# Value products of heads 25 to 27 in one stretch, in the load with the last K but one

## The chip, the core and the metric

The kernel runs on one NeuronCore of one Trainium2 chip. The metric is device time in microseconds (us) of one execution; lower is better. Five engines work side by side, each through its own list of instructions in program order: PE (TensorE, matrix products into PSUM; "PEld" is its weight load), DVE (VectorE, element-wise work and reductions), ACT (ScalarE, copies and activations), POOL (GpSimd, reductions over partitions) and SP (SyncE, which here only issues the DMA transfers). Semaphores make an instruction wait for another engine or for a transfer.

## The reference

One decode step for two batch rows: attention over the last 2048 positions of a KV cache with 32 heads of 128, plus a gated feed-forward block, both on the same normalised input. Cut to what matters:

```python
# B=2, Sq=1, D=512, 32 heads, Dh=128, W=2048 cached positions used, F=1376
xn = layernorm(x)
q  = (xn @ wq)                                  # per head 128 numbers
scores = einsum("bhqd,bhkd->bhqk", q, k) * Dh**-0.5
p  = softmax(scores)
o  = einsum("bhqk,bhkd->bhqd", p, v)            # "PV"
A  = o.reshape(B, 1, 32*128) @ wo
Bf = ((xn @ w_gate) * (xn @ w_up)) @ w_down
out = x + A + Bf
```

All data are float32. Nearly all bytes are K and V: 2 MB for each of K and V of one head, 159.5 MB in all. Each byte is used once.

## The kernel before

**The stream.** The host lays everything out as one stream, in the order in which the kernel reads it. `blocks()` cuts the stream into loads. A large load fills one of three SBUF buffers of 128 x 15872 words (`step0`, `step1`, `step2`; in the rows also `step_49`, `step_50`, `step_51`), and the loads take the buffers in turn. SP issues the transfers into a buffer when everything that lay there has been used (`done` counts the fields of a load, `pump` issues the next). Each transfer waits only for the instructions that touched the columns that it writes. All transfers are in SP's one list, in order.

**The loads that matter here.** They are the last ones of the stream:

- the load in `step1` with K of heads 28 and 29, and among others the first five eighths of V of head 25;
- the load in `step2` with K of head 30 ("the load with the last but one K"): the last three eighths of V of head 25, `wo` of head 25, V and `wo` of heads 26 and 27;
- the load in `step0` with K of head 31, V and `wo` of head 28, and two pieces of `w_down`;
- into `step1`, two transfers of 2304 KB: V and `wo` of head 29, then V and `wo` of head 30;
- into `step2`, four transfers: V of head 31 (2048 KB, over the columns of K of head 30), `wo` of head 31 with three pieces of `w_down` (1024 KB, over the last V of head 25 and `wo` of head 25), and two more with the rest of `w_down` (512 and 256 KB, over V of head 26).

**One head.** DVE multiplies K by the broadcast query (`products`) and reduces (`sums`, `maxima`); POOL takes the maximum over partitions; ACT makes the exponentials (`weights`, tile `p`, six buffers); POOL sums them; DVE takes the reciprocal. On PE then come three steps, which the text calls PV, pick and wo:

- **PV** (`weigh`): eight matmuls per head, 16 columns of weights, 512 columns of V each. Four of them write four different 32-row groups of one PSUM bank, so four can run at once. There are two banks, `o_ps0` and `o_ps1`, used in turn. Two heads can share a bank (heads 23 and 24 before, 26 and 27 here); head 25 is by itself. `copy_out` lets ACT copy the bank to SBUF (`o_sb`, two buffers).
- **pick** (`transpose`): four matmuls that turn `o_sb` and pick each head's rows, with only 2 or 4 moving columns against 128 x 128 weights, into PSUM tile `tr`; ACT then scales the result by the reciprocal into `oT` (four buffers). All picks share one PSUM bank, so a pick waits until ACT has read the one before.
- **wo** (`project_o`): one matmul of 512 columns into the sum `acc`.

A matmul in float32 is two instructions in the trace, so eight matmuls of PV are "x16" there.

**Filler.** `keep_busy(n)` is a matmul of n columns on fixed data into a PSUM bank that nobody reads (`spare`, which is the bank `q0`). It computes nothing. It stands where PE would otherwise wait for ACT.

**What sets the order.** Each engine runs its instructions in the order in which the code writes them. For the load with the last but one K, `values()` is called twice: on head 25's fields, then on those of heads 26 and 27. It runs PV as V's fields come, and at the end of a bank's last head copies out, picks and, when `wo` is there, projects. Behind it come, in program order: the maximum of head 30 (DVE), the product of head 31's K (DVE), PV of head 28, two matmuls of `w_down` (`down(1)`), a copy of the sum `acc` to SBUF (`acc_sb`, DVE), the sums of head 31 (DVE), pick of head 28, a filler, the copied sum put back into four row groups (`accumulate(carry, acc_sb)`), wo of head 28 in four matmuls of 128 columns, then heads 29, 30 and 31 one after the other, and the rest of `w_down`. The lines of `before.py` that call these, with H = 32 and GC = 512:

```python
last_two = [f for f in fields if f[1] in (H - 6, H - 5) or f[0] == "vp" and f[1][0] >= H - 6]
values([f for f in fields if f not in last_two])      # head 25
values(last_two, ((GC, 256), (GC,)))                  # heads 26, 27, with filler
keep_busy(GC)
...
transpose([HF], o_sb)                                 # head 28
keep_busy(256)
accumulate(carry, acc_sb)
project_o(HF)
```

All engine calls go through one helper, so every instruction of the profile has the line L243; they are told apart by tile names.

Of the kernel before, what the change touches and what calls it, by code (L numbers as in the profile page):

```python
# [15 lines left out]
B, D, H, DH, SK, F = 2, 512, 32, 128, 8192, 1376  # L16
# [15 lines left out]
GC = HG * DH  # L32
# [6 lines left out]
NV = CK // FB  # L39
# [232 lines left out]
def sliding_attention_plus_glu_kernel(  # L272
# [20 lines left out]
    tiles, used, left, got = {}, {}, {}, {}  # L293
# [3 lines left out]
    def pump():  # L297
        while todo:
            key, fields, at = todo[0]
            if key not in tiles:  # L300
                if key[0] == "f":
                    n = sum(w for _, _, w in fields)
                    tiles[key] = flow.tile([P, n], "first")
                elif not slots:
                    return
                else:
                    tiles[key] = slots.pop(0)
                used[key] = 0
            todo.pop(0)
            c0 = used[key]  # L310
            for kind, i, w in fields:
                got[kind, i] = (tiles[key][:, used[key] : used[key] + w], key)
                used[key] += w
            c1 = used[key]
            src = stream[at : at + P * pitch(fields)].rearrange("(p i) -> p i", p=P)
            sp.dma_start(tiles[key][:, c0:c1], src[:, : c1 - c0])

    def done(kind, i):
        _, key = got.pop((kind, i))
        left[key] -= 1  # L320
        if left[key] == 0 and key[0] != "f":
            slots.append(tiles.pop(key))
            pump()
# [61 lines left out]
    q_ps, s_t, mm_t, p_t, sum_t, rec_t, o_sbs, oT = {}, {}, {}, {}, {}, {}, {}, {}  # L385
# [8 lines left out]
    def side(h):  # L394

        return int(h % 3 == 0)
# [43 lines left out]
    def sums(h):  # L440
        s_t[h] = flow.ring([P, B, J], "s", 6)
        dve.tensor_reduce(s_t[h], k_of(h), axis=AX.X, op=ALU.add)
        done("k", h)

    def maxima(h):
        s = s_t[h]
        m = flow.ring([P, B], "m", 6)
        dve.tensor_reduce(m, s, axis=AX.X, op=ALU.max)
        mm = flow.ring([P, B], "mm", 6)
        pl.partition_all_reduce(mm, m, P, bass_isa.ReduceOp.max)  # L450
        mm_t[h] = mm
# [20 lines left out]
    def accumulate(lhsT, rhs, last=False):  # L472
        nonlocal n_acc
        for g in range(4):
            pe.matmul(
                acc_g[32 * g : 32 * g + M, :], lhsT, rhs[:, g * P : (g + 1) * P],
                start=(n_acc == 0), stop=last,
            )
        n_acc += 1

    def keep_busy(n):
        pe.matmul(spare[:, 0:n], mean_w, spare_in[:, 0:n], start=True, stop=True)

    def weigh(h, v, parts, first, last):


        for n, part in enumerate(parts):
            b, i = divmod(part, JG)
            pe.matmul(
                o_ps[bank][32 * i : 32 * i + 8 * B, :], p_t[h][:, b, i, :],  # L490
                v[:, FB * n : FB * (n + 1)], start=first and b == 0, stop=last and b == B - 1,
            )

    def copy_out():
        nonlocal bank
        o_sb = flow.ring([P, 4 * DH], "o_sb", 2)
        act.copy(o_sb, o_ps[bank])
        bank = 1 - bank
        return o_sb

    def transpose(heads, o_sb):
        d = tr[:, 8 + 4 * bank : 12 + 4 * bank]
        s0, s1 = side(heads[0]), side(heads[-1]) + 1
        dst = d.rearrange("p (s b) -> p s b", b=B)[:, s0:s1, :]
        for r in range(4):
            pe.matmul(
                dst, o_sb[:, r * DH : (r + 1) * DH], pick[:, r, s0:s1, :],
                start=(r == 0), stop=(r == 3),
            )
        for h in heads:  # L510
            rec = rec_t.pop(h)
            oT[h] = oT_ring[h % 4]
            for b in range(B):
                c = B * side(h) + b
                act.activation(
                    oT[h][:, RB * b : RB * b + 1], d[:, c : c + 1], AF.Copy,
                    scale=rec[:, b : b + 1],
                )

    def project_o(h):  # L520
        wo = got["wo", h][0]
        if h < HF:
            pe.matmul(acc, oT.pop(h), wo, start=(h == 0), stop=False)
        else:
            accumulate(oT.pop(h), wo)
        done("wo", h)
# [12 lines left out]
    def values(fields, busy=((), ())):  # L539
        for kind, i, _ in fields:  # L540
            if kind == "vp":
                h, p0, p1 = i
                heads = next(g for g in groups if h in g)
                weigh(h, got[kind, i][0], range(p0, p1), h == heads[0], h == heads[-1])
                done(kind, i)
                if (h, p1) == (heads[-1], NV):
                    o_sb = copy_out()
                    for n in busy[0]:
                        keep_busy(n)
                    transpose(heads, o_sb)  # L550
                    for n in busy[1]:
                        keep_busy(n)
                    ready.extend(heads)
            elif kind == "wo":
                arrived.append(i)
            while ready and ready[0] in arrived:
                project_o(ready.pop(0))
# [103 lines left out]
    spare, o_ps2 = spare_t[:, 0, :], spare_t[:, 1, :]  # L661
    products(h)
    sums(h)
    last_two = [f for f in fields if f[1] in (H - 6, H - 5) or f[0] == "vp" and f[1][0] >= H - 6]
    values([f for f in fields if f not in last_two])
    values(last_two, ((GC, 256), (GC,)))
    keep_busy(GC)
    maxima(h)
    reciprocals(h - 1)
    products(h + 1)  # L670
# [4 lines left out]
    dve.tensor_copy(acc_sb, acc)  # L675
    sums(h + 1)
    transpose([HF], o_sb)
    keep_busy(256)
    accumulate(carry, acc_sb)
    project_o(HF)  # L680
    weights(h)
# [14 lines left out]
    for k, t in enumerate((o_ps[bank], o_ps2)):  # L696
        for n in range(CK // FB):
            b, i = divmod(n, JG)
# [113 lines left out]
```

## Time and profile before

| | us |
|---|---|
| median of three runs | 381.35 |
| lowest and highest run | 380.67, 382.10 |
| the profiled execution's own time | 381.04 |
| its span, first to last instruction | 379.7 |
| PE busy | 261.7 (69%) |
| DVE busy | 295.2 (78%) |
| ACT busy | 58.2 (15%) |
| DMA engines, mean busy share of the queue that carries the stream | 97.4% |

The span is what the trace covers; the rows' times count from its start. The execution's own time is 1.34 us longer than its span (381.04 - 379.7). A row of a timeline or of the chain reads: start, duration, engine, tile that is written, and how many instructions were merged; in brackets the idle time just before and what ended it. In a table of stretches "PEclk" is the share of full speed that the TensorE clock was granted.

### The profile page before, as it was taken

What the parts mean: (1) busy time and instruction counts of PE and PEld (TensorE: products, weight loads), DVE (VectorE), ACT (ScalarE), POOL (GpSimd) and SP (SyncE); (2) the same over time, 40 slices, a digit from 0 to 9 for tenths busy, and PEclk for the clock granted to TensorE, in tenths of its full rate; (3) what the DMA queues carried; (4) which work ended last, traced back from release to release, by engine and by line L of the source; (5) the groups of instructions that cost most, each with busy time, mean ns of one, the idle gap of its engine ahead of it and who ended that gap; (6) DMA issues with size and microseconds to landing.
All of it is one profiled execution on the core that took longest, in us unless ns stands there. A gap on an engine that the chain in (4) does not pass through costs nothing.

```text
span 379.7 us, 2753 instructions
## 1 busy us (share of the span) xinstructions
PE 261.7 (69%) x1100; PEld 90.7 (24%) x1100; DVE 295.2 (78%) x147; ACT 58.2 (15%) x259; POOL 25.3 (7%) x78
## 2 busy tenths in 40 slices
PE   3167776895589168867775767880888184848997
PEld 3133124222133012211221212220222021203345
DVE  3069998992699992799999918999999099999460
ACT  1002012111021012111111111100212010201132
POOL 1000000000001000000000000000000000010010
PEclk9759696699688757886889687697689668566999
DMA  8999999999999999999999999999999999999991
GB/s 340 453 473 428 431 420 429 428 428 432 428 428 435 428 428 428 443 448 448 435 424 428 448 428 435 428 423 448 435 429 435 423 435 438 440 415 410 431 414 48
DMA packets 3950, 159.70 MB, mean 421 GB/s; under 512 B 466, under 2 KB 610, under 8 KB 994
## 3 DMA queue, kind: packets, MB, share of 16 engines
q1 hardware_dynamic: 3938, 159.54, 97.4%
q8 instruction: 8, 0.13, 0.1%
q14 instruction: 4, 0.03, 0.0%
HBM read 159.47 MB, written 0.07 MB: 420 GB/s over the span
## 4 chain that ended last, share of the span: by engine, by line
DMA 63%; PE 21%; DVE 14%; ACT 2%; issue 0%; SPq 0%
DMA step<-in_stream_dram 63%; PE o_ps L243 7%; DVE s L243 7%; DVE step L243 7%; PE q L243 6%; PE acc L243 4%; PE tr L243 3%; ACT o_sb L243 1%; ACT oT L243 1%; DVE m L243 0%; SPq L243 0%; DVE o_out L243 0%; DVE rec L243 0%; SPq L242 0%
## 5 line engine op out<-in xcount | busy, mean ns | idle before, releaser
L243 DVE TENSOR_TENSOR step<-step,q 128x4096 f32<-128x4096 f32 x31 | 136.7, 4411 | 47.3 <-DMA step<-in_stream_dram 47.3
L243 DVE TENSOR_REDUCE s<-step 128x32 f32<-128x4096 f32 x32 | 141.4, 4419 | 1.1
L243 PE MATMUL q<-step,xnb 128*128 128x512 f32 (+1 forms) x128 | 80.1, 773 | 72.6 <-DMA step<-in_stream_dram 72.6
L243 PE MATMUL o_ps<-step,p 128*16 128x512 f32 (+1 forms) x512 | 106.1, 764 | 10.2 <-DMA step<-in_stream_dram 10.2
L243 PEld LDWEIGHTS q<-step,xnb 128*128 128x128 f32 x128 | 28.7, 242 | 117.2 <-DMA step<-in_stream_dram 81.4
L243 PE MATMUL acc<-step,oT 128*9 128x512 f32 (+1 forms) x88 | 42.0, 638 | 9.1 <-ACT oT L243 9.1
L243 PE MATMUL tr<-first,o_sb 128*128 128x2 f32 (+2 forms) x198 | 29.8, 269 | 18.2 <-ACT o_sb L243 12.7
L243 PEld LDWEIGHTS o_ps<-step,p 128*16 128x16 f32 x512 | 18.8, 108 | 81.7 <-issue 69.2
L243 PEld LDWEIGHTS tr<-first,o_sb 128*128 128x128 f32 x198 | 27.6, 210 | 42.6 <-ACT o_sb L243 34.9
L243 ACT COPY o_sb<-o_ps 128x512 f32<-128x512 f32 (+1 forms) x24 | 13.8, 576 | 130.8 <-PE o_ps L243 130.8
L243 POOL PARTITION_ALL_REDUCE mm<-m x32 | 11.3, 354 | 266.5 <-DVE m L243 256.6
L243 ACT ACTIVATE nm<-mm 128x2 f32<-128x2 f32 x32 | 6.5, 203 | 142.1 <-POOL mm L243 142.1
L243 ACT ACTIVATE p<-s,nm 128x16 f32<-128x16 f32 x64 | 19.2, 300 | 1.0
L243 POOL PARTITION_ALL_REDUCE sum<-rs x32 | 12.7, 398 | 76.8 <-ACT p L243 76.8
L243 ACT ACTIVATE oT<-tr,rec 128x1 f32<-128x1 f32 x64 | 12.2, 260 | 29.1 <-PE tr L243 29.1
L243 DVE TENSOR_TENSOR step<-step,tr 128x4096 f32<-128x4096 f32 x1 | 4.4, 4422 | 15.1 <-DMA step<-in_stream_dram 15.1
L243 ACT ACTIVATION_READ_ACCUMULATOR p<-s,nm 128x1 f32 x64 | 12.0, 187 | 0.0
L243 PE MATMUL o_ps<-step,xn 128*2 128x512 f32 (+1 forms) x48 | 10.5, 569 | 0.0
L243 PEld LDWEIGHTS acc<-step,oT 128*9 128x9 f32 x88 | 4.5, 94 | 20.9 <-ACT oT L243 15.2
L243 PE MATMUL q<-xnb,mean_w 128*128 128x512 f32 (+1 forms) x18 | 8.5, 563 | 0.0
L243 DVE TENSOR_REDUCE m<-s 128x2 f32<-128x32 f32 x32 | 5.9, 186 | 1.1
L243 DVE RECIPROCAL rec<-sum 128x2 f32<-128x2 f32 x32 | 5.0, 155 | 2.2 <-POOL sum L243 2.2
(43 smaller groups left out, 38.1 us busy)
## 6 DMA issues: line engine op xcount, KB each, us to landing
step<-in_stream_dram SPq DMA_DIRECT2D x14, 7936.0 KB, 36.0
step<-in_stream_dram SPq DMA_DIRECT2D x2, 7680.0 KB, 33.2
step<-in_stream_dram SPq DMA_DIRECT2D x1, 7872.0 KB, 58.2
step<-in_stream_dram SPq DMA_DIRECT2D x1, 7808.0 KB, 39.0
step<-in_stream_dram SPq DMA_DIRECT2D x1, 4864.0 KB, 30.3
step<-in_stream_dram SPq DMA_DIRECT2D x2, 2304.0 KB, 19.5
step<-in_stream_dram SPq DMA_DIRECT2D x1, 2048.0 KB, 18.2
step<-in_stream_dram SPq DMA_DIRECT2D x1, 1024.0 KB, 20.3
```

Source lines behind the costliest of these rows:

```text
L243: made = getattr(eng, method)(*args, **kwargs)
```

## The change

In the load with the last but one K, the two calls of `values` and the filler behind them are replaced by a loop written out:

- PV of head 25 (its last three eighths), of head 26 and of head 27 come one after the other. ACT still copies a bank out when its last head is through, now both copies before any pick of these heads.
- Pick of head 25 stands behind PV of head 27, then a filler of 256 columns, then pick of heads 26 and 27. Before, fillers of 512 and 256 columns stood ahead of the pick of heads 26 and 27, and one of 512 behind it.
- wo of heads 25, 26 and 27 come together, and a filler of 256 columns behind them where one of 512 stood.
- Behind pick of head 28 the filler of 256 columns goes.

```diff
     sums(h)
-    last_two = [f for f in fields if f[1] in (H - 6, H - 5) or f[0] == "vp" and f[1][0] >= H - 6]
-    values([f for f in fields if f not in last_two])
-    values(last_two, ((GC, 256), (GC,)))
-    keep_busy(GC)
+    o_sbs = []
+    for kind, i, _ in fields:
+        if kind == "vp":
+            g, p0, p1 = i
+            single = g == H - 7
+            weigh(g, got[kind, i][0], range(p0, p1), single or g == H - 6, single or g == H - 5)
+            done(kind, i)
+            if p1 == NV and g != H - 6:
+                o_sbs.append(copy_out())
+    transpose([H - 7], o_sbs[0])
+    keep_busy(256)
+    transpose([H - 6, H - 5], o_sbs[1])
+    for g in (H - 7, H - 6, H - 5):
+        project_o(g)
+    keep_busy(256)
     maxima(h)
...
     sums(h + 1)
     transpose([HF], o_sb)
-    keep_busy(256)
     accumulate(carry, acc_sb)
```

DVE's and SP's lists are the same before and after; POOL's too. Three places of the lists of PE and ACT show what moves.

PE, from the arrival of the load with the last but one K to PV of head 28, before (`p1`, `p2`, `p3` are the weights of heads 25, 26, 27; `oT1`, `oT2`, `oT3` their picked values; `q0<-xnb` is filler):

```order
L243 MATMUL o_ps1<-step2_51,p1_58 16x512 x3
L243 MATMUL tr<-first_52,o_sb1_117 128x2 x4
L243 MATMUL acc<-step2_51,oT1_64 9x512
L243 MATMUL o_ps0<-step2_51,p2_59 16x512 x8
L243 MATMUL o_ps0<-step2_51,p3_60 16x512 x8
L243 MATMUL q0<-xnb_71,mean_w_55 128x512
L243 MATMUL q0<-xnb_71,mean_w_55 128x256
L243 MATMUL tr<-first_52,o_sb0_116 128x4 x4
L243 MATMUL q0<-xnb_71,mean_w_55 128x512
L243 MATMUL acc<-step2_51,oT2_65 9x512
L243 MATMUL acc<-step2_51,oT3_66 9x512
L243 MATMUL q0<-xnb_71,mean_w_55 128x512
```

The same place of PE after the change:

```order
L243 MATMUL o_ps1<-step2_51,p1_58 16x512 x3
L243 MATMUL o_ps0<-step2_51,p2_59 16x512 x8
L243 MATMUL o_ps0<-step2_51,p3_60 16x512 x8
L243 MATMUL tr<-first_52,o_sb1_117 128x2 x4
L243 MATMUL q0<-xnb_71,mean_w_55 128x256
L243 MATMUL tr<-first_52,o_sb0_116 128x4 x4
L243 MATMUL acc<-step2_51,oT1_64 9x512
L243 MATMUL acc<-step2_51,oT2_65 9x512
L243 MATMUL acc<-step2_51,oT3_66 9x512
L243 MATMUL q0<-xnb_71,mean_w_55 128x256
```

Pick and wo of head 25 have moved behind 16 matmuls of PV, and four fillers (1792 columns) have become two (512 columns).

PE a little later, at head 28 (`p4` are its weights, `hT` belongs to `w_down`, `oT0` is its picked value), as a piece of the difference:

```order
 L243 MATMUL o_ps1<-step0_49,p4_61 16x512 x8
 L243 MATMUL acc<-step0_49,hT_72 9x512 x2
 L243 MATMUL tr<-first_52,o_sb1_117 128x2 x4
-L243 MATMUL q0<-xnb_71,mean_w_55 128x256
 L243 MATMUL acc<-acc_sb_118,carry_54 9x128 x4
 L243 MATMUL acc<-step0_49,oT0_63 9x128 x4
```

Here only the filler goes; the matmul that needs DVE's copy `acc_sb` now follows the pick directly.

ACT at the first place, as a piece of the difference (`o_sb1` is head 25's copy, `o_sb0` that of heads 26 and 27):

```order
 L243 COPY o_sb1_117<-o_ps1 128x512
+L243 COPY o_sb0_116<-o_ps0 128x512
 L243 ACTIVATE oT1_64<-tr,rec1_111 128x1 x2
-L243 COPY o_sb0_116<-o_ps0 128x512
 L243 ACTIVATE oT2_65<-tr,rec2_112 128x1 x2
 L243 ACTIVATE oT3_66<-tr,rec3_113 128x1 x2
```

The copy of heads 26 and 27 has moved ahead of the scaling of head 25.

## Prediction

> **What bounds the kernel now.** I read the page first: the shares of the chain that ended last, then that chain's own end.
>
> ```profile
> DMA 63%; PE 21%; DVE 14%; ACT 2%; issue 0%; SPq 0%
> ```
>
> Most of the span is the stream. An edit near the end counts only if the chain there is on PE, so the last part of the chain decides:
>
> ```profile
> 295.73 45.38 DMA step<-in_stream_dram
> ...
> 341.16 1.94 PE o_ps L243 x6
> ...
> 348.01 4.07 PE o_ps L243 x29
> 352.08 1.49 PE q L243 x4
> 353.57 0.79 PE tr L243 x8
> 354.36 0.96 PE q L243 x2
> 355.32 1.82 PE acc L243 x4
> 357.14 1.06 PE q L243 x2
> 358.19 1.84 PE o_ps L243 x16
> 360.03 1.70 PE acc L243 x4
> 361.73 0.98 PE tr L243 x8
> 362.71 0.54 PE q L243 x2
> 363.25 0.67 PE acc L243 x16
> 363.92 1.72 PE o_ps L243 x16
> ...
> 368.44 0.34 PE acc L243 x8
> 368.78 1.72 PE o_ps L243 x16
> ...
> 373.25 0.86 PE o_ps L243 x16
> ...
> 376.08 1.69 PE acc L243 x56
> ```
>
> The load with the last but one K lands at 341.1. From 348.0 to 377.8 (376.08 + 1.69) the chain is PE alone, without a wait. Rows `q x2` and `q x4` are filler. So what PE does between 341 and 358, where this change lies, is paid one for one, until something else is late.
>
> What would be late next is the stream. Its last transfers, by issue (timeline of SP) and time to landing (the page's list, and for the first of the two of 2304 KB its own row):
>
> ```profile
> 341.01 0.80 SPq L243 DMA_DIRECT2D step<-in_stream_dram  x2
> 350.08 2.55 SPq L243 DMA_DIRECT2D step<-in_stream_dram  x4
> 352.19 0.43 SPq L243 DMA_DIRECT2D step<-in_stream_dram  x1
> ```
> ```profile
> step<-in_stream_dram SPq DMA_DIRECT2D x2, 2304.0 KB, 19.5
> ...
> step<-in_stream_dram SPq DMA_DIRECT2D x1, 2048.0 KB, 18.2
> ...
> step<-in_stream_dram SPq DMA_DIRECT2D x1, 256.0 KB, 20.5
> ```
> ```profile
> step<-in_stream_dram SPq DMA_DIRECT2D x1, 2304.0 KB, 17.0
> ```
> ```profile
> 352.61 4.42 DVE L243 TENSOR_TENSOR step<-step,q 128x4096 f32<-128x4096 f32 x1 [2.27 <-DMA step<-in_stream_dram]
> 361.77 0.68 DVE L243 COPY acc_sb<-acc 9x512 f32<-9x512 f32 x1 [4.74 <-PE acc L243]
> ```
>
> Landings: V of head 28 with the last K at 352.6 (the DVE product starts there); V of head 29 at 341.0 + 17.0 = 358.0; V of head 30 at 363.5 (the two take 19.5 in the middle, so 22.0 from about 341.4); V of head 31 at 350.1 + 18.2 = 368.3; the last `w_down` at 352.2 + 20.5 = 372.7. PE takes them up at 358.2, 363.9, 368.8, 373.25 and the last just before 377.8: each about five us late. That is the room, and no more.
>
> **What sets PE's speed at 341.** The granted clock, in stretches of 3.41 us:
>
> ```profile
> 308.21:311.62 3.41, 2.19 (x20) 1.12 (x19) 3.38 (x2) 1.00 (x3) 0.00 (x0) 1.00 1.03 447
> 311.62:315.04 3.42, 3.42 (x17) 0.66 (x10) 3.39 (x4) 0.90 (x5) 0.45 (x2) 0.50 0.98 427
> 277.49:280.90 3.41, 2.53 (x18) 1.16 (x10) 3.38 (x2) 0.70 (x2) 0.00 (x0) 1.00 0.99 428
> ...
> 342.34:345.76 3.42, 2.59 (x11) 1.78 (x8) 3.39 (x2) 0.96 (x4) 0.40 (x1) 0.50 0.95 410
> 345.76:349.17 3.41, 3.04 (x16) 0.65 (x17) 3.41 (x1) 0.32 (x2) 0.00 (x0) 0.50 1.11 479
> 349.17:352.58 3.41, 3.41 (x24) 0.88 (x20) 1.14 (x3) 0.41 (x1) 0.35 (x1) 1.00 0.86 362
> ```
>
> The first number is the length, the second PE's busy time; PEclk is the third from the end. It is 1.00 or 0.50 through a whole stretch: the clock changes on a fixed grid of 3.41 us. The picks alone in three of these stretches:
>
> ```profile
> 308.21:311.62 3.41, 1.05 (x8) 1.00 1.03 447
> 277.49:280.90 3.41, 1.05 (x8) 1.00 0.99 428
> 342.34:345.76 3.42, 1.87 (x8) 0.50 0.95 410
> ```
>
> Without picks, PE was busy (2.19 - 1.05) / 3.41 = 33% in the first, and the clock fell after it. It stayed full after the stretch at 277.49 with 43%. In 342.34 to 345.76 it was (2.59 - 1.87) / 3.42 = 21% and the clock didn't rise; in the next, 3.04 / 3.41 = 89%, and it did. I read it so: picks don't count, and the clock rises after a stretch that is nearly full of wide matmuls. Before, head 25's pick and the two waits around it spoil a stretch, and PE runs at half speed from 341.16 to 349.17.
>
> **The change, term by term.** The profiled execution's grid is kept. A PV of one head is 3.61 us at half clock:
>
> ```profile
> 323.07 3.61 PE L243 MATMUL o_ps<-step,p 128*16 128x512 f32 x16 [5.28 <-DMA step<-in_stream_dram]
> 343.76 1.87 PE L243 MATMUL tr<-first,o_sb 128*128 128x2 f32 x8 [0.69 <-ACT o_sb L243]
> 346.13 1.02 PE L243 MATMUL acc<-step,oT 128*9 128x512 f32 x1 [0.50 <-ACT oT L243]
> ```
>
> That is two rounds of four matmuls, 1.80 a round; at full clock the chain has 1.72, 0.86 a round. The stretch is five rounds (one for head 25's three matmuls, 1.94 in the chain).
>
> 1. *PV in one stretch.* PE is full from 341.16, so 342.34 to 345.76 is full and the clock rises at 345.76, not 349.17. By then (345.76 - 341.16) / 1.80 = 2.56 rounds are done; the other 2.44 take 2.10. PV ends at 347.86; before, 352.08. This takes in the two waits of 0.69 and 0.50 and the half-speed pick and wo that stood ahead.
> 2. *From there to PV of head 28.* Pick 0.79, filler 0.54, pick 0.79, three wo of 0.91 (1.82 for two) 2.73, filler 0.54: 5.39, so 353.25. Before it took 1.49 + 0.79 + 0.96 + 1.82 + 1.06 = 6.12. The fillers shrink from 3.51 to 1.08; a pick and a wo come in, 1.70. Do the ACT steps hide? The copy of heads 26 and 27 (about 0.69 with its signals) lies under head 25's pick. The second pick must wait until ACT has scaled head 25, about 0.50 behind its pick: the filler of 0.54 covers that, without it PE would wait 0.50. Scaling heads 26 and 27 lies under wo of head 25.
> 3. *Head 28.* V landed at 352.6, so no wait. PV to 355.09, `w_down` to 356.79, pick to 357.77. The copy `acc_sb` waits for DVE's product, which ends at 352.61 + 4.42 = 357.03 whatever PE does; copied by 357.71, just under the pick. Without the filler PE takes the carry (about half of the 0.67), then waits for ACT's scaling, 0.50 behind the pick: wo ends at 358.59. Of the filler's 0.54 about 0.4 is won.
> 4. *The stream takes the rest.* PV of head 29 at 358.59 (V at 358.0). Head by head 1.72 + 1.06 + 0.79 + 0.96 + 0.34 = 4.87: PE would be ready for head 30 at 363.46, V lands at 363.5. Then 1.72 + 1.06 + 0.79 + 0.54 + 0.34 = 4.45: ready at 367.95, but V of head 31 comes at 368.3. Start 368.36; what follows took 377.77 - 373.25 = 4.52; the last `w_down` at 372.7 adds about 0.1. PE ends at 373.0 instead of 377.77.
>
> DVE's sums of head 31 end at 357.7 + 4.4 = 362.1, far ahead of 368.3. On SP nothing moves in the list, but the transfer of 1024 KB writes over `wo` of head 25, whose use moves from 347 to about 350.9; it was issued behind the one of 350.08, at about 350.5. Two transfers queue behind it. The queue holds V of heads 29 to 31 until about 368, so 0.5 us of delay costs nothing; it would cost from some 15 us on. That head 26 starts in one bank while ACT copies the other I cost at nothing; at most it costs the 0.69 that PE waited there before. From below, head 25's three matmuls leave a fourth group free, a quarter of a round or 0.45 us, if head 26 fills it. The stream's slack takes most of either, so both stay inside the forecast's own range.
>
> Sum: 377.77 - 373.0 = 4.8. Span 379.7 - 4.8 = 374.9, own time 376.3. The profiled execution (381.04) lies 0.31 under the median, so 376.6 on the median's scale: 1.2% faster.
>
> **A rule weighed.** The Trainium skill, page "TensorE: Matmul & The Clock Gate", section "Why this matters for your kernels", says the clock drops mid-kernel only for idle gaps over about 3 us between matmul bursts. The trace speaks against it: in 308.21 to 311.62 the PE had 1.22 us of idle time in all, and the clock fell. By that page head 25's pick would cost no clock and joining the stretch would win none; this would be the first rival below, and I give that rule little weight. The same page's section "What's actually happening" has the window as free-running; no run here shows another execution's grid.
>
> **Rivals.**
>
> *The clock rises no earlier than before* (349.17), since short gaps never mattered or the grid lies badly: 8.01 / 1.80 = 4.45 rounds at half speed, PV ends at 349.64, 1.78 later than forecast. The stream's slack takes 0.4 of it: 376.6 + 1.3 = 377.9. For it: only one stretch of 89% is seen here, and where the grid lies against the landing is not fixed. Against: no gap at all is left. If a full stretch just fails to fit at the start, the rise comes at most 6.4 behind the landing, PV ends 0.9 later, 377.1: inside the forecast's own range of 376.0 to 377.3.
>
> *One fall of the clock in the tail*, where less filler is left. A stretch at half speed loses 3.41 x (1 - 1.72/3.61) = 1.8: 378.4.
>
> *Slower: the fillers held the clock up.* If picks and the new waits for V bring it down after every second stretch, as 308 to 315 shows, the tail runs at (1 + 0.48) / 2 = 0.74 of its pace. Its 24.4 us of work behind 347.86 take 33.0: PE ends at 380.9, span 382.8, 384.4 on the median's scale. It decides once a stretch holds less than somewhere between 33% and 43% of wide matmuls. The leanest that I find, from 347.86 on, has filler 0.54 and 1.29 of wo: 54%. So it isn't likely.
>
> *It does not do what it says:* the stream hides everything. It would need V to be taken up on landing already; the rows show five us of room. What is left is a stream that lands later in other executions: 379.5 to 381.
>
> **How the numbers follow.** Forecast 376.6 with 70%; clock no earlier, 377.9, 13%; one fall, 378.4, 6%; the fillers needed, 384.4, 4%; hidden after all, 4%; a stream that ends some 1 us earlier, 3%. The runs before spread by 0.7 to either side. Range 375.5 to 378.8. A measurement here can tell about 0.5%, 1.9 us. Faster by more: 0.91; within: 0.05; slower: 0.04.
>
> **What would show it.** Right: o_ps without a gap from the landing for some 6.7 us; PEclk full about 3.4 earlier, counted from the landing; PV of head 28 some 12 us behind the landing, not 17; short idle times "<-DMA" ahead of PV of heads 30 and 31, none before; PE's end within 0.5 of the last landing. Wrong: PEclk at 0.50 after the stretch, or the transfer of 1024 KB issued late and its landing waited for.

## The result, and the profile after

The changed kernel takes 376.03 us (median of five runs, 375.98 to 376.26) where the kernel of before took 381.46 in the same comparison: a ratio of 0.9857, with a 95% interval of 0.9841 to 0.9873. The forecast was 376.6, with a range of 375.5 to 378.8. The profiled execution took 375.98 with a span of 374.6.

PE's timeline after, from the landing of the load with the last but one K (start, duration, tile, instructions; in brackets the idle time before and what ended it):

```profile
340.61 6.37 PE L243 MATMUL o_ps<-step,p 128*16 128x512 f32 x38 [5.31 <-DMA step<-in_stream_dram]
346.91 1.05 PE L243 MATMUL tr<-first,o_sb 128*128 128x2 f32 x8
347.82 0.68 PE L243 MATMUL q<-xnb,mean_w 128*128 128x256 f32 x2
348.47 1.05 PE L243 MATMUL tr<-first,o_sb 128*128 128x4 f32 x8
349.45 2.74 PE L243 MATMUL acc<-step,oT 128*9 128x512 f32 x6
352.13 0.70 PE L243 MATMUL q<-xnb,mean_w 128*128 128x256 f32 x2
352.75 1.91 PE L243 MATMUL o_ps<-step,p 128*16 128x512 f32 x16
...
357.85 0.41 PE L243 MATMUL acc<-step,oT 128*9 128x128 f32 x8 [0.17 <-ACT oT L243]
358.07 1.90 PE L243 MATMUL o_ps<-step,p 128*16 128x512 f32 x16
...
363.05 1.91 PE L243 MATMUL o_ps<-step,p 128*16 128x512 f32 x16
...
367.89 1.06 PE L243 MATMUL o_ps<-step,p 128*16 128x256 f32 x16 [0.17 <-DMA step<-in_stream_dram]
```

All 38 instructions of PV (19 matmuls) run without a break. From the landing (340.61) PV of head 27 ends after 6.3 us, before after 10.9; PV of head 28 starts after 12.1, before after 17.0. PV of head 31 now waits for its V, by 0.17 us.

The granted clock in stretches on its grid (length, PE's busy time, ..., PEclk third from the end):

```profile
341.05:344.47 3.42, 3.42 (x20) 0.68 (x16) 3.42 (x1) 1.48 (x6) 0.47 (x2) 0.50 1.10 478
344.47:347.88 3.41, 3.41 (x31) 1.39 (x23) 3.38 (x2) 0.58 (x1) 0.00 (x0) 1.00 0.97 416
```

One stretch full of wide matmuls, and the clock is up, 3.9 us behind the landing instead of 8.0.

The end of the chain after, and SP's issues with their times to landing (the second row of issues is the last two of the first row's four):

```profile
349.55 18.29 DMA step<-in_stream_dram
...
367.89 1.06 PE o_ps L243 x16
...
370.90 1.81 PE acc L243 x56
```
```profile
349.55 2.24 SPq L243 DMA_DIRECT2D step<-in_stream_dram  x4
350.88 0.91 SPq L243 DMA_DIRECT2D step<-in_stream_dram  x2
```
```profile
step<-in_stream_dram SPq DMA_DIRECT2D x1, 1024.0 KB, 19.8
...
step<-in_stream_dram SPq DMA_DIRECT2D x1, 256.0 KB, 20.9
```

Before, PE carried the last 30 us of the chain; now a transfer does until 367.9, and PE alone is left for the last 4.8. The last transfer is the second of the row at 350.88, so issued at about 351.35; it lands at 351.35 + 20.9 = 372.2. PE ends at 372.7 (370.90 + 1.81): half a microsecond behind the stream.

### The profile page after: what moved, and what is told of

It reads as the page before. It is cut to its first block, busy times and chain, and to the rows that moved or that the text cites. A ratio compares the mean times of both kernels' runs of the same rounds, so it can differ in the third digit from the quotient of the medians.

```text
span 374.6 us, 2741 instructions
## 1 busy us (share of the span) xinstructions
PE 248.4 (66%) x1094; PEld 86.8 (23%) x1094; DVE 295.1 (79%) x147; ACT 58.1 (16%) x259; POOL 25.3 (7%) x78
## 4 chain that ended last, share of the span: by engine, by line
DMA 64%; DVE 26%; PE 7%; ACT 1%; issue 0%; SPq 0%
DMA step<-in_stream_dram 64%; DVE s L243 13%; DVE step L243 13%; PE q L243 3%; PE acc L243 2%; PE o_ps L243 2%; PE tr L243 1%; ACT o_sb L243 0%; DVE m L243 0%; ACT oT L243 0%; DVE rec L243 0%; SPq L243 0%; DVE o_out L243 0%
## 5 line engine op out<-in xcount | busy, mean ns | idle before, releaser
L243 PE MATMUL q<-step,xnb 128*128 128x512 f32 (+1 forms) x128 | 79.0, 759 | 80.5 <-DMA step<-in_stream_dram 80.5
L243 PE MATMUL o_ps<-step,p 128*16 128x512 f32 (+1 forms) x512 | 98.5, 730 | 11.2 <-DMA step<-in_stream_dram 11.2
L243 PE MATMUL acc<-step,oT 128*9 128x512 f32 (+1 forms) x88 | 39.1, 604 | 8.7 <-ACT oT L243 8.7
L243 PEld LDWEIGHTS tr<-first,o_sb 128*128 128x128 f32 x198 | 26.8, 205 | 40.6 <-ACT o_sb L243 31.3
L243 PEld LDWEIGHTS o_ps<-step,p 128*16 128x16 f32 x512 | 17.6, 107 | 78.6 <-issue 64.9
L243 POOL PARTITION_ALL_REDUCE sum<-rs x32 | 12.7, 398 | 69.1 <-ACT p L243 69.1
L243 ACT ACTIVATION_READ_ACCUMULATOR p<-s,nm 128x1 f32 x64 | 11.9, 187 | 0.0
## 6 DMA issues: line engine op xcount, KB each, us to landing
step<-in_stream_dram SPq DMA_DIRECT2D x1, 1024.0 KB, 19.8
```

The lines of the kernel that those rows point to most:

```text
L243: made = getattr(eng, method)(*args, **kwargs)
```

## Experiments

Theory: two things add up until a third, the stream, stops them. Joining PV gives PE the full clock some four us earlier and takes two waits away; the filler that goes is worth its own duration; from V of head 31 on the stream sets the end. Rivals: the filler makes the gain; idle gaps, not picks, held the clock down; PE still sets the end; a later issue makes a later landing. The times of before below are those of the same comparison, on the same chip.

### The order alone, and the filler alone

Order of the change, filler of before (against the changed kernel):

```diff
     transpose([H - 7], o_sbs[0])
+    keep_busy(GC)
     keep_busy(256)
     transpose([H - 6, H - 5], o_sbs[1])
+    keep_busy(GC)
     for g in (H - 7, H - 6, H - 5):
         project_o(g)
-    keep_busy(256)
+    keep_busy(GC)
...
     transpose([HF], o_sb)
+    keep_busy(256)
     accumulate(carry, acc_sb)
```

> The changed order of the three heads with as much filler as before the change: 512 and 256 columns ahead of the pick of heads 26 and 27, 512 behind it, 512 behind wo, 256 at head 28. Theory (the stretch gives the clock early, the filler is worth its own duration, the stream caps the rest): PV of head 27 ends some 6.3 us behind the landing of the load, as in the changed kernel; filler adds 3.51 - 1.08 = 2.4 us up to PV of head 28 and about 0.4 at head 28; 0.15 of it goes into the wait for V of head 31. So 376.0 + 2.65 = 378.7 us. Rival (the filler alone makes the gain, the order none): 381.5 us, as before the change.

Measured: 377.96 against 381.14, ratio 0.9918 (0.9903 to 0.9933). PE's timeline of its profiled execution:

```profile
347.99 1.05 PE L243 MATMUL tr<-first,o_sb 128*128 128x2 f32 x8
...
355.85 1.91 PE L243 MATMUL o_ps<-step,p 128*16 128x512 f32 x16
```

From the end of PV of head 27 to PV of head 28 it took 7.86, in the changed kernel 5.84: the filler cost 2.0, not 2.4. The two fillers that the changed kernel keeps took 0.65 and 0.62 there, not 0.54 each, and its second pick took 0.98 ahead of wo, where here it takes 0.81 ahead of a filler. That, and the lower time of before in this comparison (381.14, not 381.46), is the 0.7 by which the expected 378.7 missed.

One thing expected did not come in this profile: PV of head 27 ended 7.3 behind the landing (340.68 to 347.99), not 6.3, because the clock rose as late as 5.9 behind it. This execution was the longest of the five, 378.76.

Order of before, filler of the change (against the kernel of before):

```diff
-    values(last_two, ((GC, 256), (GC,)))
-    keep_busy(GC)
+    values(last_two, ((256,), ()))
+    keep_busy(256)
...
     transpose([HF], o_sb)
-    keep_busy(256)
     accumulate(carry, acc_sb)
```

> The order of before, with the changed kernel's amount of filler: 256 columns ahead of the pick of heads 26 and 27, 256 behind wo, none at head 28. Theory: the clock still rises some 8 us behind the landing, PV of head 27 ends about 10.9 behind it. From there to PV of head 28: 0.69 (filler inside the wait for the copy) + 0.79 + 0.50 + 1.82 + 0.54 = 4.34 instead of 6.11, and 0.4 at head 28: 381.5 - 2.2 = 379.3 us. Rival (the filler makes the whole gain): 376.0 us. If neither the filler nor the order matters alone: 381.5.

Measured: 379.49 against 381.14, ratio 0.9952 (0.9937 to 0.9967); expected were 379.3.

The order alone brings 3.2 us, the filler alone 1.65; together 4.8, and the whole change brought 4.7 and 5.4 in its two comparisons. So neither part makes the gain alone, and their sum agrees with the whole as well as the two comparisons agree with each other. Since the stream cuts the whole off, it is not shown that the parts would add up without it. PE's timeline of the filler run at the same place:

```profile
340.47 1.90 PE L243 MATMUL o_ps<-step,p 128*16 128x512 f32 x6 [5.55 <-DMA step<-in_stream_dram]
343.06 1.87 PE L243 MATMUL tr<-first,o_sb 128*128 128x2 f32 x8 [0.70 <-ACT o_sb L243]
345.44 1.02 PE L243 MATMUL acc<-step,oT 128*9 128x512 f32 x1 [0.50 <-ACT oT L243]
...
352.42 0.70 PE L243 MATMUL q<-xnb,mean_w 128*128 128x256 f32 x2
...
354.77 1.89 PE L243 MATMUL acc<-step,oT 128*9 128x512 f32 x4 [0.50 <-ACT oT L243]
```

Without the joined stretch the pick runs 1.87 at half speed, PV of head 27 ends only at 352.4, 11.9 behind the landing (expected 10.9), and a wait of 0.50 for ACT comes back where filler stood. Removing 3.5 us of filler and putting 1.1 back therefore did not win 2.4 there but 1.3: from the end of PV of head 27 to PV of head 28 it took 357.21 - 352.42 = 4.79, before 358.12 - 352.01 = 6.11. The other 0.3 was won at head 28.

### Do idle gaps or picks hold the clock down?

The kernel of before, with filler in the two waits around head 25's pick ("wide" are all matmuls but the picks):

```diff
-    values([f for f in fields if f not in last_two])
+    values([f for f in fields if f not in last_two], ((256,), (256,)))
```

> Before the change, with a filler of 256 columns in each of the two waits around head 25's pick, so that PE has no idle time from the landing on. Theory (picks do not count for the clock, only wide matmuls do, and a stretch must be nearly full of them): the pick of 1.87 us at half speed still spoils one or two stretches, the clock rises no earlier than 7.9 us behind the landing; two fillers of 1.07 at half speed take the place of waits of 0.69 and 0.50: +0.95, 382.4 us. Rival (idle gaps hold the clock down, a pick counts as busy): the clock rises 3.0 to 6.4 us behind the landing, 380.0 to 380.8 us.

Measured: 381.07 against 381.14, ratio 0.9988 (0.997 to 1.0007). Its stretches, and the picks alone in the second:

```profile
339.73:343.15 3.42, 2.72 (x8) 0.77 (x9) 3.39 (x4) 1.48 (x6) 0.75 (x2) 0.50 1.18 512
343.15:346.56 3.41, 3.41 (x15) 2.33 (x18) 3.38 (x2) 0.41 (x2) 0.00 (x0) 0.50 0.90 388
346.56:349.97 3.41, 3.41 (x20) 0.68 (x16) 3.00 (x3) 0.00 (x0) 0.35 (x1) 0.50 0.96 416
349.97:353.39 3.42, 3.42 (x21) 1.00 (x14) 1.05 (x1) 0.59 (x1) 0.00 (x1) 1.00 0.95 401
```
```profile
343.15:346.56 3.41, 1.71 (x8) 0.50 0.90 388
```

From 343.15 to 346.56 PE is busy without a break, half of it with picks, and the clock does not rise. From 346.56 it is busy with wide matmuls, and it does. Idle gaps are not needed to hold it down: picks count less than their busy time.

How much less, the twelve profiles of this case show as a whole, cut on their grids into some 1180 stretches from 30 us on. Here are two stretches at full clock, each with the one behind it (the first from the changed kernel's profile, with picks; the second from this run's, without any), and the picks of the first:

```profile
269.38:272.79 3.41, 2.50 (x15) 1.09 (x14) 3.38 (x2) 0.76 (x3) 0.00 (x0) 1.00 0.94 410
272.79:276.21 3.42, 3.13 (x10) 0.54 (x11) 3.39 (x4) 0.54 (x4) 0.35 (x1) 0.50 1.07 464
254.40:257.81 3.41, 1.43 (x4) 0.36 (x2) 3.38 (x4) 0.72 (x5) 0.35 (x1) 1.00 1.12 484
257.81:261.23 3.42, 0.00 (x0) 0.00 (x0) 3.39 (x2) 0.17 (x2) 0.40 (x1) 1.00 0.94 408
```
```profile
269.38:272.79 3.41, 1.06 (x8) 1.00 0.94 410
```

In the first PE is busy 2.50 / 3.41 = 73% and the clock falls; in the second it is busy 42% and the clock stays. Without picks both hold 42%: (2.50 - 1.06) / 3.41 and 1.43 / 3.41. In all twelve profiles every stretch at full clock with over 43% of wide work kept the clock and every one under 39% lost it, and between 39 and 43% both happen, with picks and without. So picks count for nothing that can be seen here. At half clock every stretch with over 83% brought the clock up and none under 79% did. Whether it is the few moving columns that make a pick not count, or the weight load beside them, no run separates.

The Trainium skill, page "TensorE: Matmul & The Clock Gate", section "Why this matters for your kernels", gives idle gaps of more than about 3 us between bursts of matmuls as what to avoid so that throughput does not drop. That nothing else holds the clock down is the prediction's reading, not the page's words. The run with filled waits has no idle gap behind the landing and stays at half clock for 9.5 us, so here avoiding gaps was not enough.

The expected 382.4 missed by 1.3. Two of the twelve runs took 378.38 and 378.39, but the ten others, 380.5 to 381.9, have a median of 381.3, so these two are the smaller part. Before took 0.3 less in this comparison than the 381.46 that I had started from, and the fillers made the way from the landing to wo of head 25 longer by 0.6, not 0.95 (345.97 - 340.43 = 5.54, before 346.13 - 341.16 = 4.97); the rest is open.

A grid would explain the two short runs: PV of head 25 and the first filler make 2.8 us of wide work (340.43 to 343.27), 83% of a stretch, which now and then fills one far enough ahead of the pick. To test it, the work ahead of the pick was made longer:

```diff
-    values([f for f in fields if f not in last_two])
+    values([f for f in fields if f not in last_two], ((GC,), (256,)))
```

> Before the change, with 512 columns of filler ahead of head 25's pick and 256 behind it (the run with both waits filled had 256 and 256, and two of its twelve runs took 378.4 us, ten 380.5 to 381.9). Theory (a grid stretch nearly full of wide matmuls, over 82%, lifts the clock; it must fit ahead of the pick): wide work ahead of the pick grows from 3.0 to 4.1 us, so such a stretch fits in (4.07 - 2 x 0.7 x 0.9) / 3.41, that is 40% to 60% of the executions instead of some 20%. Two groups of times: about 379 where the clock rises ahead of the pick, about 382 where it doesn't. Rival (the two short runs had another cause): one group near 382, or the same one in six.

The formula in the expectation gives 82% as it is written, not 40 to 60%. Counting the positions of the grid at which one stretch holds enough wide work gives (4.07 + 3.41 - 2 x 0.82 x 3.41) / 3.41 = 55% for a need of 82%, and 39% for a need of 90%.

Measured: 380.36 against 381.4, ratio 0.9985 (0.9959 to 1.001). But no run is near the middle: six of twelve took 378.8 to 379.3, six 381.4 to 383.0. The profiled execution is one of the short ones (stretches, then PE's timeline):

```profile
340.22:343.63 3.41, 2.99 (x8) 0.78 (x9) 3.38 (x4) 1.48 (x6) 0.76 (x2) 0.50 0.95 411
343.63:347.04 3.41, 3.41 (x28) 1.68 (x27) 3.38 (x2) 0.41 (x2) 0.00 (x0) 1.00 0.92 399
```
```profile
340.64 1.90 PE L243 MATMUL o_ps<-step,p 128*16 128x512 f32 x6 [6.01 <-DMA step<-in_stream_dram]
342.47 1.68 PE L243 MATMUL q<-xnb,mean_w 128*128 128x512 f32 x2
343.99 0.95 PE L243 MATMUL tr<-first,o_sb 128*128 128x2 f32 x8
```

2.99 / 3.41 = 88% of wide work up to 343.63 lifted the clock, and the pick then ran in 0.95 instead of 1.71. Two groups, half and half, as the grid has it; six of twelve against two of twelve are too few runs to show the share by themselves. That the long runs are those in which the grid lay worse is inferred; none of them was profiled.

### What sets the end now?

The changed kernel once more, with three variants on the same chip (before: 380.85).

> The changed kernel again, beside the three that follow. Theory (the stream sets its end): time within 0.2 us from run to run, 1.4% under the kernel of before; the granted clock rises at another distance behind the landing (3.0 to 6.4 us) and the end is still within 0.6 us of the last landing. Rival (PE still sets the end): the end moves with the place where the clock rises, by up to 0.9 us.

Measured: 376.19 (376.04 to 376.3), ratio 0.9878 (0.9863 to 0.9893). The clock rose 4.0 behind the landing, nearly as in the first profile, so this profile alone doesn't tell the two theories apart; the variants do.

The filler behind head 28's pick put back:

```diff
     transpose([HF], o_sb)
+    keep_busy(256)
     accumulate(carry, acc_sb)
```

> The changed kernel with the filler of 256 columns behind head 28's pick put back. Theory: 0.54 of filler takes the place of a wait of 0.17, so PE is 0.37 later at V of heads 29 to 31; the wait for V of head 31 (0.17) swallows part: 0.2 us more than the changed kernel on the same chip. Rival (this filler's whole 0.54 counts): 0.5 us more.

Measured: 376.19, ratio 0.9878 (0.9861 to 0.9894).

The two new fillers out:

```diff
     transpose([H - 7], o_sbs[0])
-    keep_busy(256)
     transpose([H - 6, H - 5], o_sbs[1])
     for g in (H - 7, H - 6, H - 5):
         project_o(g)
-    keep_busy(256)
```

> The changed kernel without its two new fillers of 256 columns; the tail from head 28 on keeps its filler. Theory: a wait of 0.50 stands in the place of the first, the second's 0.54 goes, and PE waits as much longer for V of heads 30 and 31: no gain, within 0.15 us of the changed kernel. The clock stays up: the leanest stretch, behind PV of head 27, has some 50% wide matmuls or more. Rival (PE sets the end): 0.5 us less.

Measured: 376.03, ratio 0.9874 (0.9859 to 0.9889). In its timeline the time won is waited away:

```profile
349.13 1.05 PE L243 MATMUL tr<-first,o_sb 128*128 128x4 f32 x8 [0.50 <-ACT oT L243]
...
363.22 1.91 PE L243 MATMUL o_ps<-step,p 128*16 128x512 f32 x16 [0.18 <-DMA step<-in_stream_dram]
...
368.04 1.06 PE L243 MATMUL o_ps<-step,p 128*16 128x256 f32 x16 [0.15 <-DMA step<-in_stream_dram]
```

More filler and less filler give the same time. In these profiles the clock rose 2.8 us (filler put back) and 4.9 us (two out) behind the landing, and the end did not follow. PE no longer sets it. The expected 0.2 more for the filler was not seen; in that profile PE still waited 0.17 and 0.16 for V, since its clock came early.

wo of head 25 moved further back, behind the carry:

```diff
-    for g in (H - 7, H - 6, H - 5):
+    for g in (H - 6, H - 5):
         project_o(g)
...
     accumulate(carry, acc_sb)
+    accumulate(oT.pop(H - 7), got["wo", H - 7][0])
+    done("wo", H - 7)
     project_o(HF)
```

> The changed kernel with wo of head 25 moved still later, behind the carry of head 28 (as four matmuls of 128 columns), so that the transfer of 1024 KB over its columns is issued some 7 us later, at about 357.6 instead of 350.5. Theory (the queue holds work until V of head 31 has landed, some 368): the transfer and the two behind it land when they did, 370.3 to 372.2; wo in four small matmuls is 0.5 us shorter on PE, which the stream swallows: within 0.15 us of the changed kernel. Rival (a transfer lands some 20 us behind its issue): the last landing moves to about 379, the time to about 383 us.

Measured: 376.19, ratio 0.9879 (0.9865 to 0.9894). SP's issue of the transfer of 1024 KB, and the page's times to landing:

```profile
358.89 0.33 SPq L243 DMA_DIRECT2D step<-in_stream_dram  x1
```
```profile
step<-in_stream_dram SPq DMA_DIRECT2D x1, 1024.0 KB, 11.7
...
step<-in_stream_dram SPq DMA_DIRECT2D x1, 256.0 KB, 12.7
```

Issued 8.4 us later than in the changed kernel (350.51), it landed at 358.9 + 11.7 = 370.6 instead of 370.3. The time to landing is mostly queueing; the rival falls. But that the kernel's time did not move is in part luck: in this profile the clock fell once (below), PE waited for no V, and its end lay 0.5 behind the last landing (359.72 + 12.7 = 372.4) by its own work.

### Is the filler in the tail needed?

The changed kernel without any filler from this load on:

```diff
     transpose([H - 7], o_sbs[0])
-    keep_busy(256)
...
-    keep_busy(256)
     maxima(h)
...
-    value(H - 3, ((GC,), (GC,)))
+    value(H - 3, ((), ()))
...
-    keep_busy(GC)
     transpose([H - 2], o_sb)
-    keep_busy(256)
```

> The changed kernel without any filler from the load with the last but one K to the end. Theory: where a filler goes, a wait for ACT of 0.5 to 0.7 us stands, so nothing is lost directly and the stream still sets the end: 376.0 us if the clock stays up. But per head of some 5 us only about 2.1 are wide matmuls (39%), and a stretch between PV of two heads can hold under 30%; where the trace of before fell was 33%, where it stayed 43%. So the clock should fall at least once behind PV of head 28, and cost up to 1.8 us each time: 376.8 to 378.4 us. Rival (only idle gaps of about 3 us let the clock fall): PEclk stays at 1.00, 375.9 to 376.0 us.

Measured: 377.7 (377.36 to 380.25) against 381.14, ratio 0.9928 (0.99 to 0.9956): some 1.6 us more than the changed kernel took in the other comparisons (376.03 and 376.19). Four of the six runs took 377.4 to 378.0; the two others, 380.1 and 380.3, lie above the expected 376.8 to 378.4, and neither was profiled. Stretches, and the picks in two of them:

```profile
358.38:361.79 3.41, 2.20 (x21) 1.09 (x13) 3.22 (x3) 1.00 (x3) 0.23 (x2) 1.00 1.00 429
361.79:365.21 3.42, 2.88 (x20) 0.61 (x24) 0.65 (x2) 0.90 (x5) 0.62 (x2) 0.50 1.01 433
365.21:368.62 3.41, 2.19 (x28) 1.31 (x24) 0.00 (x0) 1.00 (x3) 0.00 (x0) 1.00 0.93 394
368.62:372.03 3.41, 3.41 (x35) 1.32 (x26) 0.00 (x0) 0.43 (x2) 0.00 (x0) 0.50 0.69 279
```
```profile
358.38:361.79 3.41, 1.05 (x8) 1.00 1.00 429
365.21:368.62 3.41, 1.05 (x8) 1.00 0.93 394
```

Two stretches with (2.20 - 1.05) / 3.41 = 34% and 33% of wide matmuls, and behind each the clock falls, though no idle gap of PE in them was over 0.71 us. The rival, by which it stays, falls. PV of head 30, behind the first fall, took 3.01 us instead of 1.91. Filler that covers a wait of 0.6 us is worth little by itself; in a tail of picks and short waits it holds the clock.

### Before, once more

> The kernel of before, profiled once more. Theory (a fixed grid of 3.41 us lies at another distance from the landing in each execution): the clock rises between 7.8 and 11.3 us behind the landing, PV of head 27 ends 10.9 to 12.5 us behind it, PE waits for no landing after that, and PE's end stands 25.7 us behind PV of head 27. Rival (the clock follows the work alone): again 8.0 and 10.9.

Measured: 381.15 against 381.4, ratio 0.9995 (0.9981 to 1.0009). PE's timeline:

```profile
340.62 1.90 PE L243 MATMUL o_ps<-step,p 128*16 128x512 f32 x6 [7.28 <-DMA step<-in_stream_dram]
...
351.73 1.56 PE L243 MATMUL q<-xnb,mean_w 128*128 128x512 f32 x4
```

From the landing at 340.62 the clock rose after 8.5 us and PV of head 27 ended after 11.1; PE ended at 377.5, 25.7 behind that. The rival's 8.0 and 10.9 are close, so this one profile decides little; but with the filler run's 11.9 the same work in the same order has ended 10.9, 11.1 and 11.9 behind its landing.

## Why the prediction was right

*What bounds:* right. PE set the end before; taking work off it moved the end until V of head 31 was waited for.

*Step 1, PV in one stretch:* right in mechanism. Forecast was the end of PV 6.70 behind the landing, measured 6.30; the clock rose 3.9 behind it, not 4.6, since this execution's grid lay better.

*Step 2, to PV of head 28:* 5.39 forecast, 346.91 to 352.75 = 5.84 measured. Each piece from start to start was up to 0.2 longer than the chain's durations before (pick 0.91 and 0.98 for 0.79, filler 0.65 and 0.62 for 0.54; wo 2.68 for 2.73). ACT's steps hid as forecast: no wait stands ahead of the second pick or the first wo.

Step 1 came 0.40 early and step 2 0.45 late, so that PV of head 28 started 12.14 behind the landing where 12.09 was forecast is luck.

*Step 3, head 28:* 5.34 forecast, 358.07 - 352.75 = 5.32 measured, with the wait of 0.17 for ACT's scaling that I put at about 0.15.

*Step 4, the stream takes the rest:* right, and shown from both sides by the runs with more and with less filler. PE's end lies 0.5 behind the last landing; forecast 0.3. PE waited 0.17 for V of head 31 where the sum has 0.41; the wait for V of head 30, 0.04 in the sum, doesn't appear in the first profile (the runs with more and with less filler show 0.17 and 0.18).

*SP:* the transfer of 1024 KB was issued at 350.5 (I had put it at about 350.9) and cost nothing; even 8.4 us more cost nothing.

*The 0.6 us between 376.6 and 376.03:* the shift of 0.31 to the median's scale was one half. It held for before, whose runs spread more, probably with the clock's grid, but the changed kernel ends with the stream and its profiled execution lies 0.05 from its median. The other half is the landing: the profile on which I worked has it at 341.16 in PE's rows; the eleven others have it between 340.43 and 340.85. The last landing came 0.5 earlier than forecast (372.2, not 372.7), and PE ended 0.2 further behind it.

*Rivals:* in every profile with the joined stretch the clock rose 2.8 to 5.9 us behind the landing, so "no earlier" fell. A fall of the clock is real: it came with all filler gone, and once in the run with the late wo of head 25, where filler and two wo alone stood behind the picks. Its stretch, the one behind, and the picks alone in the first:

```profile
346.95:350.36 3.41, 2.91 (x17) 1.81 (x17) 2.72 (x3) 1.31 (x7) 0.36 (x1) 1.00 1.05 449
350.36:353.78 3.42, 3.42 (x9) 0.79 (x11) 1.51 (x1) 0.00 (x0) 0.00 (x0) 0.50 0.92 394
```
```profile
346.95:350.36 3.41, 1.57 (x13) 1.00 1.05 449
```

(2.91 - 1.57) / 3.41 = 39% fell, inside the 33 to 43% that I had given as the point of decision. In the changed kernel wo of head 25 stands in that place, and neither of its two profiles shows a fall: until PE's end their leanest stretch holds 64% of wide matmuls. The slower rival, a clock that falls again and again, did not come: in the changed kernel's profiles PEclk stays at 1.00 from its rise to PE's end.

## What to carry to other kernels

Count the engine's wide matmuls per clock stretch, not its busy time: a step with two moving columns against a full weight load keeps PE busy and still costs the clock. Put such steps together, behind the long matmuls, and let real work stand where filler stood; check with a run without filler whether the rest of it is still needed. Before counting on a saving, subtract each transfer's landing from the moment at which it is taken up: the smallest difference is about all that can be won, here 4.9 us, and 4.7 and 5.4 were measured in two comparisons.

## What the hardware showed that was not expected

The point of decision lies between 39 and 43% of wide matmuls in a stretch of 3.41 us when the clock falls and between 79 and 83% when it rises, with picks left out of the count. Since the same PV takes 3.61 us at half clock and 1.72 at full clock, that is about the same amount of work both times. The grid can make one kernel two: with 512 columns of filler ahead of the pick, half the runs took about 379 and half about 382, with nothing between 379.4 and 381.3. That the grid is the cause is inferred. And a queued transfer's time to landing says little of the transfer: 1024 KB took 19.8 us when issued at 350.5 and 11.7 when issued at 358.9.
